# Gate/up of a SwiGLU block in 256-column chunks, partly issued between the groups of the inverse transform before it

## Chip, cores, metric

One core of a Trainium2 chip. The metric is device time in microseconds (us) of one execution; lower is better. A kernel repeated on one chip scatters mostly by 0.5%, at most by 0.8%, around its median, so versions are compared through ratios that were measured in the same rounds.

## The reference, cut to what matters

```python
# S = 2048 rows, D = 640, F = 1728, all bfloat16
h  = x + A(layernorm(x), k, v, ...)      # A: long convolution, done here with DFT matrices
xn = layernorm(h)
h2 = h + (silu(xn @ w_gate) * (xn @ w_up)) @ w_down
```

The convolution is computed as two forward transforms, products in the frequency domain and an inverse transform, all as matmuls against cosine and sine tables. Then comes the feed-forward block. Only the part from the inverse transform on is changed.

## The kernel before

The kernel places each instruction on one engine's in-order queue and lists the semaphore values that it waits for. PE does matmuls, DVE the elementwise work, ACT the activations. PE writes its results to PSUM, a memory in banks, from which DVE and ACT read them; a bank can be used again when they have. The inverse transform has 16 groups, one for each tile of 128 rows. One group is 32 matmuls (384 and 256 columns in turn), then `y_output` on DVE with one Sqrt on ACT, then, two groups later, five PE transposes of the normalized rows:

```python
for par in range(2):
    for tb in range(NT):                                   # 16 groups
        banks, ytok = inverse_group(gi, par, tb)           # PE: 32 matmuls
        if len(pend) >= 2:
            hn_transposes(*pend.pop(0), [4, 5, 6, 7], ...) # PE: 5 transposes, DVE: 1 copy
        y_output(qi, par, tb, banks, ytok)                 # DVE, one Sqrt on ACT
        pend.append((par, tb))
...
def y_output(...):                       # ... cut to the order of the DVE queue
    q  = (x - mean) * rstd               # 1
    d  = kv * D                          # 2
    s  = psum + d                        # 3, 4: frees the PSUM banks of the inverse
    o  = q * s ; h = x + o               # 5, 6
    bn_stats, bn_stats, bn_aggr          # 7 to 9
    Sqrt on ACT, then reciprocal         # 10
    hn = (h - mean2) * rstd2             # 11
```

After all 16 groups the feed-forward runs in two halves of 1024 rows. Gate/up tiles are 512 columns wide, with one PSUM bank for gate and one for up, three such pairs in turn. A down half starts only when all products of its half are there:

```python
def gate_up_half(par, ...):
    for fb in range(NFB):                # 14 blocks of features, the last one of 64
        for c in range(NUC):             # 2 tiles of 512 columns
            # PE: 5 gate matmuls in bank bG, 5 up matmuls in bank bU, alternating
            t_sg = act.op(... Sigmoid ..., deps=[lastG, ...])
            t_gs = dve.op(... gate * sigmoid ..., deps=[t_sg, ...])
            t_gu = dve.op(... up * that ..., deps=[t_gs, lastU])
...
gate_up_half(0) ; down_half(0) ; gate_up_half(1) ; down_half(1)
```

## Time and profile before

| | before |
|---|---|
| median at the time of the prediction | 491.54 us (4 runs) |
| inverse transform on PE | 204.6 to 290 us |
| gate/up and down, first half | 290.5 to 392 us |
| gate/up and down, second half | 392 to 487 us |

In the profile PE is the matmul engine. These lines of the kernel matter: L742 the inverse matmuls, L767 the DVE adds that free the banks of the inverse, L793 the transposes, L797 their copy, L848 and L850 the gate and up matmuls, L856 the sigmoid, L858 and L861 the two products, L891 the down matmuls, L777 the Sqrt.

The first lines of the page of the kernel before give the span and each engine's busy time:

```profile
span 490.2 us, 6781 instructions
...
PE 420.5 (86%) x2710; PEld 261.1 (53%) x2710; DVE 328.2 (67%) x624; ACT 133.6 (27%) x298; POOL 0.3 (0%) x5
```

The table by stretches, kernel before. The columns are the stretch, its length, the busy time of PE, PEld (weight loads), DVE, ACT and POOL with the number of instructions, the granted clock of PE as a share of full speed (0.50 is half clock), and DMA's share and GB/s. The stretches are the inverse, the hand-over to gate/up, the first down half and the second gate/up half:

```profile
204.60:290.50 85.90, 77.52 (x582) 54.89 (x582) 67.74 (x172) 4.12 (x14) 0.00 (x0) 0.98 0.32 109
290.50:302.00 11.50, 7.26 (x36) 3.17 (x37) 8.99 (x22) 3.45 (x6) 0.00 (x0) 1.00 0.01 1
...
358.30:392.00 33.70, 33.66 (x224) 21.30 (x224) 6.23 (x14) 0.00 (x0) 0.00 (x0) 0.95 0.10 35
392.00:454.80 62.80, 60.82 (x282) 27.49 (x281) 39.58 (x58) 16.70 (x28) 0.00 (x0) 1.00 0.01 4
```

In the hand-over PE is busy only 7.26 of 11.5 us. The clock of 0.95 in the first down half means a piece at half clock: (1 - 0.95) x 33.7 is 1.7 us lost.

The waits of PE from 204 us on, kernel before (total, times, longest). The first line is the stage before, which the change doesn't touch:

```profile
PE ps L742 <- DVE r_stage L693: 26.5, 1, 26.5
PE ps L742 <- DVE r_x L767: 7.9, 13, 0.8
PE ps L891 <- DVE tabs L861: 4.0, 2, 2.0
PE ps L848 <- DVE tabs L861: 2.9, 1, 2.9
PE ps L848 <- DVE r_k L797: 1.3, 1, 1.3
PE ps L848 <- DVE r_x L767: 0.6, 1, 0.6
```

Besides that first line PE waits 16.7 us: 7.9 in the inverse (DVE frees the banks too late), 4.8 at the hand-over, 4.0 before the two down halves. That is all that better overlap could win at the full clock. PE starts one inverse group every 5.37 us but has only 4.35 us of inverse matmuls and 0.28 us of transposes to do in it.

Two groups of DVE instructions with their mean time in ns give the cost of a narrower product: 691 at 512 columns, and 415 for an add of 256 columns that also reads PSUM (kernel before, groups by form):

```profile
L858 DVE TENSOR_TENSOR r_kpl<-ps,r_kpl 128x512 bf16<-128x512 f32 x52 | 36.0, 691 | 37.6 <-ACT r_kpl L856 37.6
...
L899 DVE TENSOR_TENSOR r_x<-ps,kvt 128x256 bf16<-128x256 f32 x16 | 6.6, 415 | 0.0
```

The timeline of ACT before the first Sqrt (start, duration, instruction) shows a table load of 1.28 us:

```profile
83.37 1.28 ACT L520 ACT_TABLE_LOAD   x1
84.66 0.32 ACT L520 ACTIVATE sqv<-lnstat,epsv 128x16 f32<-128x16 f32 x1
```

That Sqrt needs the last result of the convolution's input stage, which DVE finishes at 84.1 us. The load starts before that. It does not wait for the activation's operand.

### The profile page before, as it was taken

The page shows a single profiled execution, that of the slowest core. Times are in us where ns is not written, and L with a number is a line of the kernel's source. Part 1 is how long each engine was busy: PE and PEld are TensorE (multiplying, and loading weights), DVE is VectorE, ACT ScalarE, POOL GpSimd, SP SyncE. Part 2 cuts the span into 40 slices and gives each one's busy share as a digit, 9 for nine tenths or more (in the row PEclk, how much of TensorE's full clock was granted, in tenths as well). Part 3 has the DMA queues.
Part 4 walks back from the last instruction along what each step waited for, and adds up shares of the span by engine and source line. Part 5 has one row for each costly group of instructions (what it writes and reads, how often), then busy time and mean ns, then how long its engine had stood idle before and what let it go on. Part 6 is the DMA issues. An engine that isn't in the chain of part 4 may idle for free.

```text
span 490.2 us, 6781 instructions
## 1 busy us (share of the span) xinstructions
PE 420.5 (86%) x2710; PEld 261.1 (53%) x2710; DVE 328.2 (67%) x624; ACT 133.6 (27%) x298; POOL 0.3 (0%) x5
## 2 busy tenths in 40 slices
PE   2589998999998850398998987999989999999897
PEld 1456775677775530166666653444446644444564
DVE  0789998096499999748888888666622256666222
ACT  0843435655665550000000003222200022222000
POOL 0000000000000000000000000000000000000000
PEclk9888999899999985599999999999989999999999
DMA  8999710000000000294110100000001100000011
GB/s 296 348 350 345 226 66 2 0 1 1 1 1 1 0 1 1 68 408 134 41 28 27 30 25 1 1 1 0 1 14 42 40 15 0 2 0 1 27 41 40
DMA packets 24271, 32.22 MB, mean 66 GB/s; under 512 B 2800, under 2 KB 17968, under 8 KB 24240
## 3 DMA queue, kind: packets, MB, share of 16 engines
q1 hardware_dynamic: 21168, 25.16, 15.8%
q10 hardware_dynamic: 3072, 6.64, 3.6%
q8 instruction: 21, 0.34, 0.3%
q14 instruction: 10, 0.08, 0.1%
HBM read 29.16 MB, written 2.62 MB: 65 GB/s over the span
## 4 chain that ended last, share of the span: by engine, by line
PE 49%; DVE 39%; SPq 4%; issue 3%; ACT 2%; DMA 1%; DVEq 0%
PE ps L891 13%; PE ps L848 12%; DVE r_x L629 12%; PE ps L850 12%; PE ps L574 9%; SPq L311 4%; PE ps L742 3%; DVE r_x L767 3%; DVE r_stage L629 2%; DVE r_x L770 2%; DVE kvt L771 2%; DVE st L773 2%; DVE r_k L779 1%; DVE st L417 1%; DMA r_stage<-in_A_k_dram 1%
## 5 line engine op out<-in xcount | busy, mean ns | idle before, releaser
L848 PE MATMUL ps<-r_k,r_kpl 128*128 128x512 bf16 (+1 forms) x280 | 106.2, 379 | 4.8 <-DVE tabs L861 2.9
L850 PE MATMUL ps<-r_k,r_kpl 128*128 128x512 bf16 (+1 forms) x280 | 106.1, 379 | 0.0
L742 PE MATMUL ps<-r_stage,tabs 128*128 128x384 bf16 x480 | 71.7, 304 | 34.4 <-DVE r_stage L693 26.5
L742 PEld LDWEIGHTS ps<-r_stage,tabs 128*128 128x128 bf16 x480 | 46.6, 99 | 54.7 <-DVE r_stage L693 26.9
L574 PE MATMUL ps<-r_k,tabs 128*128 128x384 bf16 x480 | 70.0, 311 | 6.3 <-ACT r_k L543 4.3
L574 PE MATMUL ps<-kvt,tabs 128*128 128x384 bf16 x480 | 67.7, 304 | 7.0 <-ACT r_x L588 4.8
L891 PE MATMUL ps<-r_x,tabs 128*128 128x384 bf16 x448 | 66.0, 305 | 4.0 <-DVE tabs L861 4.0
L858 DVE TENSOR_TENSOR r_kpl<-ps,r_kpl 128x512 bf16<-128x512 f32 (+1 forms) x56 | 38.7, 691 | 40.9 <-ACT r_kpl L856 40.9
L856 ACT ACTIVATE r_kpl<-ps 128x512 bf16<-128x512 f32 (+1 forms) x56 | 33.2, 597 | 120.3 <-PE ps L848 120.3
L574 PEld LDWEIGHTS ps<-r_k,tabs 128*128 128x128 bf16 x480 | 48.4, 101 | 27.2 <-ACT r_k L543 4.5
L574 PEld LDWEIGHTS ps<-kvt,tabs 128*128 128x128 bf16 x480 | 47.4, 99 | 27.0 <-ACT r_x L588 5.4
L891 PEld LDWEIGHTS ps<-r_x,tabs 128*128 128x128 bf16 x448 | 41.9, 99 | 28.4 <-issue 8.9
L899 DVE TENSOR_TENSOR r_x<-ps,kvt 128x384 bf16<-128x384 f32 (+1 forms) x32 | 14.2, 486 | 53.9 <-PE ps L891 53.9
L629 DVE TENSOR_TENSOR r_x<-r_x 128x1280 bf16<-128x1280 bf16 x40 | 31.5, 820 | 25.5 <-ACT r_k L588 13.4
L848 PEld LDWEIGHTS ps<-r_k,r_kpl 128*128 128x128 bf16 (+1 forms) x280 | 27.6, 99 | 38.9 <-DVE tabs L861 4.2
L629 DVE TENSOR_TENSOR r_x<-r_x,r_kpl 128x2560 bf16<-128x2560 bf16 x32 | 46.2, 1486 | 0.3
L850 PEld LDWEIGHTS ps<-r_k,r_kpl 128*128 128x128 bf16 (+1 forms) x280 | 27.6, 99 | 31.8
L584 ACT ACTIVATE r_kpl<-ps,sck 128x384 bf16<-128x384 f32 x64 | 28.5, 528 | 44.1 <-PE ps L574 44.1
L861 DVE TENSOR_TENSOR tabs<-ps,r_kpl 128x512 bf16<-128x512 f32 (+1 forms) x56 | 38.7, 691 | 1.9
L777 ACT ACTIVATE sqv<-lnstat,epsv 128x1 f32<-128x1 f32 x16 | 4.7, 294 | 110.4 <-DVE lnstat L775 76.0
L584 ACT ACTIVATE r_x<-ps 128x384 bf16<-128x384 f32 x64 | 25.6, 454 | 33.3 <-PE ps L574 30.7
L588 ACT ACTIVATE r_x<-ps,tw 128x384 bf16<-128x384 f32 (+1 forms) x64 | 31.3, 565 | 0.0
(58 smaller groups left out, 249.2 us busy)
## 6 DMA issues: line engine op xcount, KB each, us to landing
r_stage<-in_A_k_dram SPq DMA_DIRECT2D x15, 320.0 KB, 5.1
r_k<-in_A_ssm_k_dram SPq DMA_DIRECT2D x5, 512.0 KB, 5.8
r_stage<-in_A_q_dram SPq DMA_DIRECT2D x8, 320.0 KB, 4.2
r_stage<-in_A_v_dram SPq DMA_DIRECT2D x8, 320.0 KB, 4.5
r_x<-in_A_q_dram SPq DMA_DIRECT2D x16, 160.0 KB, 2.2
out_dram<-r_x SPq DMA_DIRECT2D x16, 160.0 KB, 1.8
r_kpl<-in_B_w_gate_dram ACTq DMA_DIRECT2D x1, 2160.0 KB, 8.6
r_kpl<-in_B_w_up_dram ACTq DMA_DIRECT2D x1, 2160.0 KB, 13.9
```

Source lines behind the costliest of these rows:

```text
L311: return e.op_inc(lambda g, d=dst, s=src: g.dma_start(d, s), sem, 16, deps=deps)
L574: t.matmul(o, l, r, start=st, stop=sp_),
L584: atok = act.op(lambda a, o=dst, s=src, sc=sc: a.activation(out=o, in_=s, func=ACTF.Copy, scale=sc), deps=[last[gi]] + list(extra_act_deps))
L588: atok = act.op(lambda a, o=sdst[:, ch0:ch0 + cw], s=src[0:npart], sc=ssc: a.activation(out=o, in_=s, func=ACTF.Copy, scale=sc), deps=list ...
L629: tt = lambda o, a, b2, op, dd: dve.op(lambda v: v.tensor_tensor(out=o, in0=a, in1=b2, op=op), deps=dd)
L742: lasts[c] = pe.op(lambda t, o=o, l=lhsT, r=r, st=first, sp_=(cnt > nmm - NCH): t.matmul(o, l, r, start=st, stop=sp_), deps=deps if (first ...
L848: lastG = pe.op(lambda t, o=oG, l=lg, r=rhs, st=st, sp_=sp_: t.matmul(o, l, r, start=st, stop=sp_), deps=deps if dti == 0 else ())
L850: lastU = pe.op(lambda t, o=oU, l=lu, r=rhs, st=st, sp_=sp_: t.matmul(o, l, r, start=st, stop=sp_))
L856: t_sg = act.op(lambda a, o=sgb, s=oG: a.activation(out=o, in_=s, func=ACTF.Sigmoid), deps=[lastG, gu_pair_done.get(pidx - 3)])
L858: t_gs = dve.op(lambda v, o=gsb, s=oG, g=sgb: v.tensor_tensor(out=o, in0=s, in1=g, op=ALU.mult), deps=[t_sg, gu_pair_done.get(pidx - 3)])
L861: t_gu = dve.op(lambda v, o=dstgu, s=oU, g=gsb: v.tensor_tensor(out=o, in0=s, in1=g, op=ALU.mult), deps=[t_gs, lastU] + guT_war_deps)
L891: last = pe.op(lambda t, o=o, l=lhsT, r=r, st=first, sp_=(ft == NFB - 1): t.matmul(o, l, r, start=st, stop=sp_), deps=deps if (first and c ...
```

## The change

The intent is to give PE something to do while the inverse is bound by DVE. Gate/up is cut into eight chunks of 256 rows, and the rows of a chunk are ready as soon as two row tiles are transposed. In each inverse group from the fourth on, two gate/up blocks (one feature block of gate and up, 256 columns) are issued. After the inverse, one down chunk and 14 gate/up blocks alternate, with the blocks about 12 ahead of the down chunk that needs them. Gate and up now share one PSUM bank.

```diff
-    TUW = min(512, H)
+    TC = min(256, H)              # rows of a chunk; SBC = 2 row tiles
...
+        pair_banksets = [(b_, b_) for b_ in [4, 5, 6]]
...
+        def gu_emit(ci):          # next block of chunk ci; cut
+                oG = bank32(bG, 0, TC)[0:mrows]
+                oU = bank32(bU, TC, TC)[0:mrows]       # same bank, other half
+                lastG = pe.op(... t.matmul(o, l, r, start=st, ...))
+                lastU = pe.op(... t.matmul(o, l, r, start=False, ...))
+            t_sg = act.op(... Sigmoid ..., deps=[lastU, prev3])
+            t_gs, t_gu = dve.op(...), dve.op(...)
...
-        def y_output(qi, par, tb, banks, ytok):
+        def y_output(qi, par, tb, banks, ytok, between=lambda: None):
                 bank_rd[banks[c]] = t_s
+            between()             # here: between adds 3, 4 and product 5
...
+        GU_PER_GROUP = 2
+        NGSLOT = 2                # products of two chunks are held at a time
...
+                    hn_transposes(ppar, ptb, [7], tri[0])
+                t_h, t_hn = y_output(qi, par, tb, banks, ytok, between=lambda: emit_some_gu(GU_PER_GROUP))
...
+        while next_down < n_chunks:
+            # any block of this chunk still missing is emitted first (cut)
+            down_chunk(next_down)
+            downs_emitted[0] = next_down + 1
+            while pend:
+                ...
+                hn_transposes(ppar, ptb, [7], tri[0])
+            emit_some_gu(NFB)
+            next_down += 1
```

Two accumulations are open in one bank at once. The Trainium skill ("PSUM — Partial Sum Buffer", The four PSUM rules) says that only the first matmul issued there may carry the start flag, and that the second group, in other columns, overwrites at its first matmul without it. The change follows that.

More of the change, by code (lines that the diff above doesn't have):

```diff
@@ L139, in bass_sequential_preLN__ssm_conv_h3__swiglu_ffn__prompt_kernel @@
     assert FL in (32, 64, 128)
-    TUW = min(512, H)
-    assert H % TUW == 0
-    NUC = H // TUW
+    TC = min(256, H)
+    assert H % TC == 0 and TC % P == 0
+    NCC = H // TC
+    SBC = TC // P
+    TUW = TC
     half = D // 2
@@ L189, in bass_sequential_preLN__ssm_conv_h3__swiglu_ffn__prompt_kernel @@
         stab = tabs[:, NT * H:2 * NT * H].rearrange("p (t h) -> p t h", t=NT)
-        assert NFB * H <= 2 * NT * H
-        guT = tabs[:, 0:NFB * H].rearrange("p (f u) -> p f u", f=NFB)
         kvt = sb("kvt", [P, 2, NT, D], bf)
@@ L245, in bass_sequential_preLN__ssm_conv_h3__swiglu_ffn__prompt_kernel @@
         assert yoff <= sz_k, (yoff, sz_k)
-        sz_kpl = max(NF * 4 * D, 2 * NDT * F + 6 * TUW)
+        sz_kpl = max(NF * 4 * D, 2 * NDT * F + 6 * TUW + NFB * TC)
         r_kpl = sb("r_kpl", [P, sz_kpl], bf)
@@ L253, in bass_sequential_preLN__ssm_conv_h3__swiglu_ffn__prompt_kernel @@
         gsbuf = [r_kpl[:, sgoff + (3 + i) * TUW:sgoff + (4 + i) * TUW] for i in range(3)]
+        gcoff = sgoff + 6 * TUW
+        guC = [None, r_kpl[:, gcoff:gcoff + NFB * TC].rearrange("p (f u) -> p f u", f=NFB)]
         xt_elems = 2 * 6 * D + 2 * 4 * D + 2 * 2 * D + 4 * D
@@ L284, in bass_sequential_preLN__ssm_conv_h3__swiglu_ffn__prompt_kernel @@
             yoff2 += D
+        if yoff2 + NFB * TC <= r_x.shape[1]:
+            guC[0] = r_x[:, yoff2:yoff2 + NFB * TC].rearrange("p (f u) -> p f u", f=NFB)
+            yoff2 += NFB * TC
+        else:
+            guC[0] = sb("guC0", [P, NFB, TC], bf)[:, :, :]
         ps = es.enter_context(nc.psum_tensor("ps", [P, 8 * BANK], f32))
@@ L722, in bass_sequential_preLN__ssm_conv_h3__swiglu_ffn__prompt_kernel, with inverse_group @@
         ytmp_prev = {0: [], 1: []}
-        def inverse_group(gi, par, tb):
-            banks = [(gi % 2) * 2, (gi % 2) * 2 + 1]
+        def inverse_group(gi, par, tb, force_banks=None):
+            banks = force_banks if force_banks is not None else [(gi % 2) * 2, (gi % 2) * 2 + 1]
             deps = list(inv_deps_all)
@@ L806, in bass_sequential_preLN__ssm_conv_h3__swiglu_ffn__prompt_kernel @@
         tri = [0]
-        gi = 0
-        for par in range(2):
-            for tb in range(NT):
-                qi = gi
-                banks, ytok = inverse_group(gi, par, tb)
-                if len(pend) >= 2:
-                    ppar, ptb = pend.pop(0)
-                    hn_transposes(ppar, ptb, [4, 5, 6, 7], tri[0])
-                    tri[0] += 1
-                t_h, t_hn = y_output(qi, par, tb, banks, ytok)
-                h_tok[(par, tb)] = t_h
-                pend.append((par, tb))
-                if qi + NXR < len(y_order):
-                    x_reload(qi + NXR)
-                gi += 1
@@ L823, in bass_sequential_preLN__ssm_conv_h3__swiglu_ffn__prompt_kernel @@
-        gu_pair_done = {}
-        sg_prev = [None] * 3
-        pair_banksets = [(0, 1), (4, 5), (6, 7)]
-        def gate_up_half(par, pidx_start, tr_interleave):
-            pidx = pidx_start
-            u_half0 = par * H
-            hnT_deps = [hnT_tok[(par, tb)] for tb in range(NT)]
-            tri = 0
-            for fb in range(NFB):
-                mrows = P if fb < NFB - 1 else FL
-                for c in range(NUC):
-                    bset = pair_banksets[pidx % 3]
-                    bG, bU = bset
-                    deps = [t_wg, t_wu] + hnT_deps + [gu_pair_done.get(pidx - 3)]
-                    deps += [bank_rd.get(bG), bank_rd.get(bU), tr_bank_rd.get(bG), tr_bank_rd.get(bU)]
-                    lastG = lastU = None
-                    for dti in range(NDT):
-                        lg = Wg_sb[:, dti, fb * P:fb * P + mrows]
-                        lu = Wu_sb[:, dti, fb * P:fb * P + mrows]
-                        rhs = hnT[:, dti, u_half0 + c * TUW:u_half0 + (c + 1) * TUW]
-                        oG = bank32(bG, 0, TUW)[0:mrows]
-                        oU = bank32(bU, 0, TUW)[0:mrows]
-                        st = dti == 0
-                        sp_ = dti == NDT - 1
-                        lastG = pe.op(lambda t, o=oG, l=lg, r=rhs, st=st, sp_=sp_: t.matmul(o, l, r, start=st, stop=sp_),
-                                      deps=deps if dti == 0 else ())
-                        lastU = pe.op(lambda t, o=oU, l=lu, r=rhs, st=st, sp_=sp_: t.matmul(o, l, r, start=st, stop=sp_))
-                    sgi = pidx % 3
-                    sgb = sgbuf[sgi][0:mrows, :]
-                    gsb = gsbuf[sgi][0:mrows, :]
-                    oG = bank32(bG, 0, TUW)[0:mrows]
-                    oU = bank32(bU, 0, TUW)[0:mrows]
-                    t_sg = act.op(lambda a, o=sgb, s=oG: a.activation(out=o, in_=s, func=ACTF.Sigmoid),
-                                  deps=[lastG, gu_pair_done.get(pidx - 3)])
-                    t_gs = dve.op(lambda v, o=gsb, s=oG, g=sgb: v.tensor_tensor(out=o, in0=s, in1=g, op=ALU.mult),
-                                  deps=[t_sg, gu_pair_done.get(pidx - 3)])
-                    dstgu = guT[0:mrows, fb, c * TUW:(c + 1) * TUW]
-                    t_gu = dve.op(lambda v, o=dstgu, s=oU, g=gsb: v.tensor_tensor(out=o, in0=s, in1=g, op=ALU.mult),
-                                  deps=[t_gs, lastU] + guT_war_deps)
-                    gu_pair_done[pidx] = t_gu
-                    bank_rd[bG] = t_gs
-                    bank_rd[bU] = t_gu
-                    pidx += 1
-                if tr_interleave is not None and tri < len(tr_interleave):
-                    tr_interleave[tri]()
-                    tri += 1
-            while tr_interleave is not None and tri < len(tr_interleave):
-                tr_interleave[tri]()
-                tri += 1
-            return pidx
@@ L875, in down_half @@
-        def down_half(par, qstart):
-            q = qstart
-            gdeps = [gu_pair_done[k] for k in gu_pair_done]
-            wdep = [t_wd, t_wd2]
-            for tb in range(NT):
-                banks = [(q % 2) * 2, (q % 2) * 2 + 1]
-                deps = gdeps + wdep + [bank_rd.get(banks[0]), bank_rd.get(banks[NCH - 1])] + [tr_bank_rd.get(banks[0]), tr_bank_rd.get(banks[NCH - 1])]
+        chunk_list = [(par, cc) for par in range(2) for cc in range(NCC)]
+        gu_done = {}
+        pair_banksets = [(b_, b_) for b_ in [4, 5, 6]]
@@ new lines, in bass_sequential_preLN__ssm_conv_h3__swiglu_ffn__prompt_kernel, with chunk_ready @@
+        NSET = len(pair_banksets)
+        pidx_c = [0]
+        down_done = {}
+        gu_next_fb = {}
+        obuf_free = [None, None]
+        q_c = [0]
+        def chunk_ready(ci):
+            par, cc = chunk_list[ci]
+            return all((par, SBC * cc + sb) in hnT_tok for sb in range(SBC))
+        def gu_emit(ci):
+            fb = gu_next_fb.get(ci, 0)
+            if fb >= NFB:
+                return False
+            gu_next_fb[ci] = fb + 1
+            par, cc = chunk_list[ci]
+            pidx = pidx_c[0]
+            pidx_c[0] += 1
+            mrows = P if fb < NFB - 1 else FL
+            u0 = par * H + cc * TC
+            hdeps = [hnT_tok[(par, SBC * cc + sb)] for sb in range(SBC)]
+            bG, bU = pair_banksets[pidx % NSET]
+            slot = ci % 2
+            deps = [t_wg, t_wu] + hdeps + [gu_done.get((pidx - NSET, None))]
+            deps += [bank_rd.get(bG), bank_rd.get(bU), tr_bank_rd.get(bG), tr_bank_rd.get(bU)]
+            lastG = lastU = None
+            for dti in range(NDT):
+                lg = Wg_sb[:, dti, fb * P:fb * P + mrows]
+                lu = Wu_sb[:, dti, fb * P:fb * P + mrows]
+                rhs = hnT[:, dti, u0:u0 + TC]
+                oG = bank32(bG, 0, TC)[0:mrows]
+                oU = bank32(bU, TC, TC)[0:mrows]
+                st = dti == 0
+                sp_ = dti == NDT - 1
+                lastG = pe.op(lambda t, o=oG, l=lg, r=rhs, st=st, sp_=sp_: t.matmul(o, l, r, start=st, stop=sp_, skip_group_check=True),
+                              deps=deps if dti == 0 else ())
+                lastU = pe.op(lambda t, o=oU, l=lu, r=rhs, sp_=sp_: t.matmul(o, l, r, start=False, stop=sp_, skip_group_check=True))
+            sgi = pidx % 3
+            sgb = sgbuf[sgi][0:mrows, :]
+            gsb = gsbuf[sgi][0:mrows, :]
+            oG = bank32(bG, 0, TC)[0:mrows]
+            oU = bank32(bU, TC, TC)[0:mrows]
+            prev3 = gu_done.get((pidx - 3, None))
+            t_sg = act.op(lambda a, o=sgb, s=oG: a.activation(out=o, in_=s, func=ACTF.Sigmoid), deps=[lastU, prev3])
+            t_gs = dve.op(lambda v, o=gsb, s=oG, g=sgb: v.tensor_tensor(out=o, in0=s, in1=g, op=ALU.mult), deps=[t_sg, prev3])
+            dstgu = guC[slot][0:mrows, fb, :]
+            t_gu = dve.op(lambda v, o=dstgu, s=oU, g=gsb: v.tensor_tensor(out=o, in0=s, in1=g, op=ALU.mult),
+                          deps=[t_gs, lastU, down_done.get(ci - 2)])
+            gu_done[(pidx, None)] = t_gu
+            gu_done[(ci, fb)] = t_gu
+            bank_rd[bG] = t_gs
+            bank_rd[bU] = t_gu
+            return True
@@ new lines, in down_chunk @@
+        def down_chunk(ci):
+            par, cc = chunk_list[ci]
+            slot = ci % 2
+            gdeps = [gu_done[(ci, fb)] for fb in range(NFB)]
+            wdep = [t_wd, t_wd2]
+            last = None
+            for sb in range(SBC):
+                tb = SBC * cc + sb
+                q = q_c[0]
+                q_c[0] += 1
+                banks = [2 * sb, 2 * sb + 1] if SBC * 2 <= 4 else [(q % 2) * 2, (q % 2) * 2 + 1]
+                deps = gdeps + wdep + [bank_rd.get(b_) for b_ in banks] + [tr_bank_rd.get(b_) for b_ in banks]
@@ L882, in down_half @@
                 first = True
-                last = None
-                u0 = tb * P
+                u0 = sb * P
                 for ft in range(NFB):
                     krows_ = P if ft < NFB - 1 else FL
-                    lhsT = guT[0:krows_, ft, u0:u0 + P]
+                    lhsT = guC[slot][0:krows_, ft, u0:u0 + P]
                     for c, (ch0, cw) in enumerate(chunks):
@@ L903, in down_half, with emit_some_gu @@
                 obuf_free[q % 2] = otok
-                q += 1
-            return q
-        obuf_free = [None, None]
-        guT_war_deps = []
-        tr1 = [lambda t=t, k=k: hn_transposes(t[0], t[1], [2, 3], k) for k, t in enumerate(pend)]
-        pend = []
-        pidx = gate_up_half(0, 0, tr1)
-        q = down_half(0, 0)
-        guT_war_deps = []
-        pidx = gate_up_half(1, pidx, None)
-        q = down_half(1, q)
+            down_done[ci] = last
+        gi = 0
+        n_chunks = len(chunk_list)
+        cur_gu = [0]
+        GU_PER_GROUP = 2
+        NGSLOT = 2
+        downs_emitted = [0]
+        def emit_some_gu(nmax):
+            n = 0
+            while n < nmax and cur_gu[0] < n_chunks:
+                ci = cur_gu[0]
+                if ci >= downs_emitted[0] + NGSLOT or not chunk_ready(ci):
+                    break
+                if gu_emit(ci):
+                    n += 1
+                else:
+                    cur_gu[0] += 1
+            return n
+        for par in range(2):
+            for tb in range(NT):
+                qi = gi
+                banks, ytok = inverse_group(gi, par, tb)
+                if len(pend) >= 2:
+                    ppar, ptb = pend.pop(0)
+                    hn_transposes(ppar, ptb, [7], tri[0])
+                    tri[0] += 1
+                t_h, t_hn = y_output(qi, par, tb, banks, ytok, between=lambda: emit_some_gu(GU_PER_GROUP))
+                h_tok[(par, tb)] = t_h
+                pend.append((par, tb))
+                if qi + NXR < len(y_order):
+                    x_reload(qi + NXR)
+                gi += 1
+        next_down = 0
+        while next_down < n_chunks:
+            while gu_next_fb.get(next_down, 0) < NFB:
+                assert chunk_ready(next_down)
+                gu_emit(next_down)
+            if cur_gu[0] <= next_down:
+                cur_gu[0] = next_down + 1
+            down_chunk(next_down)
+            downs_emitted[0] = next_down + 1
+            while pend:
+                ppar, ptb = pend.pop(0)
+                hn_transposes(ppar, ptb, [7], tri[0])
+                tri[0] += 1
+            emit_some_gu(NFB)
+            next_down += 1
         sp.wait([s_out[0].cur(), s_out[1].cur()])
```

## The prediction

> **What bounds the kernel now.** Only the part from the inverse transform on (204.6 to 490.2 us) changes. Read from the chain of waits and the timeline:
> - inverse transform, 204.6 to about 296 us: bound by DVE. Each group takes 5.37 us, paced by DVE; PE needs 4.35 plus five transposes at 56 ns, and waits 0.6 to 0.8 per group. The hand-over to gate/up costs PE 2.9 and 1.3 us more.
> - gate/up twice, about 61 us each: bound by PE, matmuls of 512 columns 215 ns apart; DVE is busy 63% of it.
> - down twice, about 33 us each: bound by PE, 4.02 us per row tile. Before each, PE waits 2.0 us for the last gating product; half clock after one of them costs 1.7 us.
>
> **What the change does.** Gate and up go to 256 columns, in eight chunks of rows, and two feature blocks are issued per inverse group from the fourth group on: 26 of the 112 blocks, 28 us of PE work, move into the DVE-bound stage.
>
> Costs, from the trace:
> - PE: 256-column matmuls in the inverse start every 109 ns with their weight loads hidden: 1.09 us a block; gate/up grows by 2 to 4 us in all.
> - DVE: a product from PSUM takes 691 ns at 512 columns and 415 ns at 256 (the adds of that size). Two blocks add about 1.5 us per group; DVE becomes 5.37 + 1.5 = 6.87 us, PE 4.35 + 0.28 + 2.18 = 6.8. They almost balance.
> - ACT: Sqrt and Sigmoid now alternate. The Trainium skill ("ScalarE: Activation LUTs", What ACT_TABLE_LOAD costs) gives 1283 ns plus a drain of 1380 per switch. The trace shows 1283 and no drain before the sigmoids (the load starts 0.02 us after Sqrt ends). I expect about 26 loads, 33 us of ACT, but hidden: the load before the first Sqrt starts at 83.4 us, before its DVE input is ready at 84.1, so loads don't wait for the activation's operand, and ACT idles over 2 us before each Sqrt.
> - One PSUM bank per gate/up pair, three sets: release takes about 1.7 us, below the 2.2 us of the other two sets. No PE stall.
>
> **The sum.** Fourth group at 230.4 us, a stall of PE before it (225.1 to 229.7, waiting for the second transposed tile), perhaps followed by half clock (1.5 us); last group near 314 us; 1.5 us around the last transposes. Then 86 blocks (95 us) and 14 row tiles (56 us), one wait of 1.8 us before the last chunk instead of two, and the same 3.2 us tail: span about 484, time **485.5 us**, range 479 to 493. Faster by over 2%: 0.24; within 2%: 0.69; slower: 0.07.
>
> **What would show it.** Inverse groups 6.8 to 7.2 us apart; 256-column starts 109 ns apart; about 28 table loads, few on the chain; chain in the interleaved stage mixed PE and DVE; PE continuous from about 327 us to the last chunk; DVE busy up about 11 us.
>
> **What would make it wrong.** Table loads that wait for the operand: +1.3 us per group, total about 500; with the skill's drain more. PE stalls from three banks, or DVE and PE delaying each other: +5 us. More half clock through short idle times (the skill, "TensorE: Matmul & The Clock Gate", Part 1: idle PE is throttled; here 3.4 us at 0.5 after one wait).

## The result and the profile after

The changed kernel ran in 483.92 us (median of 11 runs, 480.42 to 485.71; a twelfth run, 486.26, outside this median) against 491.78 us before (16 runs). The ratio is 0.9827, with a 95% interval of 0.980 to 0.985. Ratios here and below are the mean time of one kernel's fast runs over that of the other's of the same rounds, so they are not quite the ratio of the quoted medians. The gain is 1.7%: within 2%, and within the predicted range of 479 to 493. The outputs are right.

In the changed kernel L749 is the inverse, L774 its adds, L801 and L805 the transposes and their copy, L854 and L856 gate and up, L863 the sigmoid, L864 and L866 the products, L894 down, L785 the Sqrt. The first lines of its page:

```profile
span 483.9 us, 8166 instructions
...
PE 422.8 (87%) x3270; PEld 316.2 (65%) x3270; DVE 342.9 (71%) x736; ACT 176.6 (37%) x380; POOL 0.3 (0%) x5
```

The waits of PE in the changed kernel, from 205 us on:

```profile
PE ps L749 <- DVE r_stage L700: 24.9, 1, 24.9
PE ps L854 <- DVE r_k L805: 4.3, 1, 4.3
PE ps L894 <- DVE r_kpl L866: 1.5, 1, 1.5
PE ps L801 <- DVE r_k L805: 1.1, 1, 1.1
PE ps L749 <- DVE r_x L774: 0.9, 1, 0.9
```

Without the first line PE waits 7.8 us instead of 16.7. The 13 waits inside the inverse, the hand-over and one of the two waits before down are gone. A new one stands at the top, 4.3 us: the first block waits for the copy of the second transposed tile, and behind it in PE's queue the next inverse group waits too.

The stretches of the changed kernel: the groups without blocks, the first group with blocks, the other twelve, and the alternating stage after the inverse:

```profile
205.90:231.00 25.10, 19.90 (x139) 13.77 (x140) 14.23 (x36) 2.17 (x4) 0.00 (x0) 0.91 0.82 298
231.00:236.40 5.40, 5.40 (x25) 3.54 (x25) 2.84 (x8) 1.40 (x3) 0.00 (x0) 0.50 0.00 0
236.40:317.60 81.20, 81.20 (x680) 63.84 (x679) 72.35 (x188) 42.50 (x59) 0.00 (x0) 1.00 0.09 24
...
327.50:470.90 143.40, 143.40 (x1200) 114.65 (x1196) 82.85 (x195) 32.53 (x85) 0.00 (x0) 1.00 0.05 16
```

In the second of these PE runs at half clock after its wait, which costs 2.7 us. In the third PE is busy for the whole stretch. DVE is nearly full too, busy 72.35 of 81.20 us: in a closer timeline its only regular wait is 0.36 us per group, for the Sqrt, as before. The groups start 6.81 us apart in PE's timeline.

The products and the two kinds of table load in the changed kernel (groups by form):

```profile
L864 DVE TENSOR_TENSOR r_kpl<-ps,r_kpl 128x256 bf16<-128x256 f32 x104 | 43.9, 423 | 23.6 <-ACT r_kpl L863 23.6
...
L863 ACT ACT_TABLE_LOAD x14 | 18.0, 1283 | 0.2
L785 ACT ACT_TABLE_LOAD x13 | 16.7, 1283 | 0.2
```

Where the loads stand, from the timeline of ACT over one group:

```profile
255.28 0.38 ACT L863 ACTIVATE r_kpl<-ps 128x256 bf16<-128x256 f32 x1 [0.34 <-PE ps L856]
256.38 0.38 ACT L863 ACTIVATE r_kpl<-ps 128x256 bf16<-128x256 f32 x1 [0.71 <-PE ps L856]
256.78 1.28 ACT L785 ACT_TABLE_LOAD   x1
260.17 0.29 ACT L785 ACTIVATE sqv<-lnstat,epsv 128x1 f32<-128x1 f32 x1 [2.11 <-DVE lnstat L783]
260.49 1.28 ACT L863 ACT_TABLE_LOAD   x1
262.09 0.38 ACT L863 ACTIVATE r_kpl<-ps 128x256 bf16<-128x256 f32 x1 [0.33 <-PE ps L856]
```

Each load starts 0.02 us after the activation before it, is over before its own activation may start, and is followed by a wait for PE or DVE. The room is not the same at both places: over the twelve groups the waits after a load are 1.8 to 2.3 us before the Sqrt, but mostly 0.3 us, and at least 0.16, before the sigmoid. 27 loads take 34.7 us of ACT and none of the critical path. A drain of 1380 ns, which the Trainium skill ("ScalarE: Activation LUTs", What ACT_TABLE_LOAD costs) adds to each switch, is not seen.

**The balance from the start of the inverse.** It lasts 285.6 us before (490.2 - 204.6) and 278.0 us after (483.9 - 205.9), 7.6 us less. To count PE's pauses in one way for both kernels, take every distance of more than 0.4 us between the starts of two successive matmuls and subtract what such a pair takes without a pause. (The waits view counts a bit less, since it lets a matmul's modelled end overlap the pause.) The sums are 19.5 us before and 8.4 us after.

| Term | us |
|---|---|
| PE's pauses | -11.1 |
| half clock: 1.7 before, 2.7 after, and 0.3 less at the very start | +0.7 |
| gate/up, from the starts of matmuls: 112 blocks of 1.107 us; before, the same work 1.082 us | +2.9 |
| down, in the same way: 63.9 in both | 0.0 |
| sum | -7.5 |

### The profile page after: what moved, and what is told of

Its sections match the earlier page's. It is cut to its first block, busy times and chain, and to the rows that moved or that the text cites. A ratio compares the mean times of both kernels' runs of the same rounds, so it can differ in the third digit from the quotient of the medians.

```text
span 483.9 us, 8166 instructions
## 1 busy us (share of the span) xinstructions
PE 422.8 (87%) x3270; PEld 316.2 (65%) x3270; DVE 342.9 (71%) x736; ACT 176.6 (37%) x380; POOL 0.3 (0%) x5
## 4 chain that ended last, share of the span: by engine, by line
PE 64%; DVE 27%; SPq 4%; issue 2%; DMA 1%; ACT 1%; DVEq 0%
PE ps L749 14%; PE ps L854 13%; PE ps L894 13%; PE ps L856 13%; DVE r_x L636 12%; PE ps L581 10%; SPq L318 4%; DVE r_stage L636 2%; DMA r_stage<-in_A_k_dram 1%; DVE st L424 1%; DVE r_stage L431 1%; DVE r_stage L433 1%; DVE r_stage L436 1%; DVE r_stage L437 1%; DVE r_stage L428 1%
## 5 line engine op out<-in xcount | busy, mean ns | idle before, releaser
L854 PE MATMUL ps<-r_k,r_kpl 128*128 128x256 bf16 (+1 forms) x560 | 126.3, 276 | 4.3 <-DVE r_k L805 4.3
L856 PE MATMUL ps<-r_k,r_kpl 128*128 128x256 bf16 (+1 forms) x560 | 126.1, 275 | 0.0
L749 PE MATMUL ps<-r_stage,tabs 128*128 128x384 bf16 x480 | 71.8, 304 | 25.8 <-DVE r_stage L700 24.9
L863 ACT ACTIVATE r_kpl<-ps 128x256 bf16<-128x256 f32 x112 | 42.9, 383 | 132.6 <-PE ps L856 132.6
L581 PE MATMUL ps<-kvt,tabs 128*128 128x384 bf16 x480 | 70.0, 310 | 8.9 <-ACT r_x L595 4.8
L749 PEld LDWEIGHTS ps<-r_stage,tabs 128*128 128x128 bf16 x480 | 47.4, 99 | 45.0 <-DVE r_stage L700 25.2
L581 PE MATMUL ps<-r_k,tabs 128*128 128x384 bf16 x480 | 68.5, 307 | 6.3 <-ACT r_k L550 4.3
L864 DVE TENSOR_TENSOR r_kpl<-ps,r_kpl 128x256 bf16<-128x256 f32 x112 | 47.3, 422 | 25.8 <-ACT r_kpl L863 25.8
L854 PEld LDWEIGHTS ps<-r_k,r_kpl 128*128 128x128 bf16 (+1 forms) x560 | 55.7, 99 | 14.9 <-issue 6.4
L856 PEld LDWEIGHTS ps<-r_k,r_kpl 128*128 128x128 bf16 (+1 forms) x560 | 55.8, 100 | 6.1
L894 PE MATMUL ps<-r_x,r_kpl 128*128 128x384 bf16 x224 | 32.3, 300 | 1.5 <-DVE r_kpl L866 1.5
L894 PE MATMUL ps<-r_x 128*128 128x384 bf16 x224 | 32.3, 300 | 0.0
L785 ACT ACTIVATE sqv<-lnstat,epsv 128x1 f32<-128x1 f32 x16 | 4.7, 294 | 71.7 <-DVE lnstat L783 37.5
L894 PEld LDWEIGHTS ps<-r_x,r_kpl 128*128 128x128 bf16 x224 | 20.8, 97 | 12.2 <-issue 3.2
```

Source lines behind the costliest of these rows:

```text
L581: t.matmul(o, l, r, start=st, stop=sp_),
L749: lasts[c] = pe.op(lambda t, o=o, l=lhsT, r=r, st=first, sp_=(cnt > nmm - NCH): t.matmul(o, l, r, start=st, stop=sp_), deps=deps if (first ...
L854: lastG = pe.op(lambda t, o=oG, l=lg, r=rhs, st=st, sp_=sp_: t.matmul(o, l, r, start=st, stop=sp_, skip_group_check=True), deps=deps if dt ...
L856: lastU = pe.op(lambda t, o=oU, l=lu, r=rhs, sp_=sp_: t.matmul(o, l, r, start=False, stop=sp_, skip_group_check=True))
L863: t_sg = act.op(lambda a, o=sgb, s=oG: a.activation(out=o, in_=s, func=ACTF.Sigmoid), deps=[lastU, prev3])
L864: t_gs = dve.op(lambda v, o=gsb, s=oG, g=sgb: v.tensor_tensor(out=o, in0=s, in1=g, op=ALU.mult), deps=[t_sg, prev3])
```

## The experiments

Ratios are against the kernel before of the same rounds; diffs are against the changed kernel unless said otherwise. The theories at the start:

- **A**: the gain is the interleaving, PE work moved into a stage bound by DVE.
- **B**, a rival: interleaving is nearly free of net gain, since its first block waits 4.3 us and then runs at half clock. The gain is the order by chunks, which removes the waits at the hand-over and before down.
- Beside these: what the narrow tiles cost, and whether the table loads are really hidden.

| Run | Median, us | Ratio (95%) |
|---|---|---|
| no interleaving | 495.17 | 1.004 (1.000 to 1.008) |
| blocks from the fifth group on | 479.43 | 0.973 (0.969 to 0.976) |
| narrow tiles alone | 494.81 | 1.004 (1.000 to 1.008) |
| table loads exposed | 500.42 | 1.016 (1.011 to 1.020) |
| ends filled | 477.11 | 0.969 (0.966 to 0.973) |
| 12 blocks in the last six groups | 489.34 | 0.994 (0.990 to 0.998) |
| 12 blocks in groups five to ten | 490.94 | 0.997 (0.993 to 1.001) |
| changed kernel again | 484.21 | 0.983 (0.980 to 0.987) |
| bridge | 488.00 | 0.989 (0.985 to 0.994) |
| blocks from the fifth group on, again | 479.33 | 0.971 (0.968 to 0.975) |
| bridge, ready in time | 483.15 | 0.982 (0.980 to 0.985) |

### No interleaving

```diff
-        GU_PER_GROUP = 2
+        GU_PER_GROUP = 0
...
+        emit_some_gu(26)          # the same blocks, right after the inverse
         next_down = 0
```

> The changed kernel, but no gate/up block is issued inside the inverse transform; the same 26 blocks follow directly after it, in the same order, so that everything later is unchanged. Theory A (the gain is the interleaving: PE work moved into the stage bound by DVE): the 26 blocks come back as 29 us behind an inverse stage of 5.37 us per group, and the time returns to that of the kernel before or more, 491 to 494 us. Theory B (read from the gaps between matmuls: most of the gain is the order by chunks, which removes the waits at the hand-over, 4 us, and before the two down stages, 4.5 us and 1.7 us of half clock, and the interleaving gives nearly nothing net, since its first block waits 4.4 us and then runs at half clock): 485 to 487 us, with inverse groups 5.37 us apart and no PE wait over 2 us except one before the last chunk.

It took 495.17 us, slightly more than the kernel before. Theory B, which I held at that point, is wrong. The waits of PE in this kernel around the hand-over:

```profile
PE ps L854 <- DVE r_x L866: 7.8, 1, 7.8
```

and the stretch after that wait:

```profile
297.30:302.70 5.40, 5.34 (x26) 3.78 (x27) 2.79 (x8) 0.77 (x2) 0.00 (x0) 0.50 0.00 0
```

The hand-over did not vanish with the order by chunks; it grew. ACT and DVE take their queues in order, so the sigmoids and products of these blocks stand behind the Sqrt and the DVE work of the last two row tiles. PE fills its three banks (3.3 us of work) and then waits 7.8 us for the first of them, after which half clock costs 2.7 us. In the kernel before, the three bank pairs held twice as much work, and its longest such wait was 2.9 us. So the interleaving earns its keep, but not only by filling idle time inside the inverse; the runs below look at the hand-over.

### Blocks from the fifth group on

```diff
-                ... between=lambda: emit_some_gu(GU_PER_GROUP))
+                ... between=lambda: emit_some_gu(GU_PER_GROUP if qi >= 4 else 0))
```

> The changed kernel, with the first blocks issued in the fifth inverse group instead of the fourth (24 blocks inside the stage instead of 26). If the 4.4 us wait of PE before its first block and the half clock after it are a loss on the critical path, as I think, the wait goes and PE runs on: 3 to 6 us less than the changed kernel, 478 to 481 us, no gap over 1.2 us between matmuls of 215 to 320 us and no stretch at half clock there. If the stage is bound by DVE from there on, so that the wait is hidden, the time stays within 1 us of the changed kernel, 483 to 485.

It took 479.43 us, as expected on the side of "the wait is on the critical path". The same kernel, repeated in later rounds, gave 0.971. One condition in the emission loop wins another 1% over the changed kernel, whose ratio is 0.983. In the trace the wait for the second transposed tile is gone. These waits of PE are left:

```profile
PE ps L801 <- DVE r_k L805: 2.1, 1, 2.1
PE ps L894 <- DVE r_kpl L866: 1.5, 1, 1.5
PE ps L749 <- DVE r_x L774: 0.6, 1, 0.6
```

The first two lie after the inverse. Up to its end no wait of PE is over 1 us, and from 208 to 317 us PE runs at full clock.

### Narrow tiles alone

The diff is against the kernel before:

```diff
-    TUW = min(512, H)
+    TUW = min(256, H)
```

> The kernel before, with gate/up in tiles of 256 columns instead of 512 and nothing else changed. This is the cost of the narrower tile by itself: 109 ns instead of 215 per matmul, and more waits of PE on DVE, 112 instead of 56 blocks: 3 to 4 us longer than the kernel before, 494 to 496 us, the two gate/up stages about 62.5 us instead of 61. If the weight loads or the gating on DVE (77 to 93 us) limited the narrow tiles, it would be over 6 us longer.

It took 494.81 us, ratio 1.004: by the ratio 1.8 us more than the kernel before, less than the 3 to 4 expected and not clear of zero (the interval starts at 0.9996). The second gate/up half, which no other effect disturbs, takes 61.3 us instead of 60.6, both with PE busy throughout. So the narrow matmuls as such cost 0.7 us per half, less than the 1.5 I expected; 256 columns are enough to hide each weight load. At the hand-over the longest wait went from 2.9 to 4.5 us and was followed by 6.1 us at half clock, while the two waits before down shrank from 4.0 to 2.7 us; I have not taken these apart further.

### Table loads exposed

```diff
             t_sg = act.op(... Sigmoid ...)
+            if gi < NT * 2 and pidx % 2 == 0:       # first block of an inverse group
+                act.op(lambda a: a.activation(out=dumv[:], in_=epsv[:], func=ACTF.Sqrt, ...))
             t_gs = dve.op(...)
```

> The changed kernel, with one dummy Sqrt of one column between the two sigmoids of each inverse group (one group in two blocks). It adds two table loads of 1.28 us and 0.3 us per group at a place where DVE waits for the second sigmoid. If the table loads are free in the changed kernel only because ACT has idle time where they fall, as predicted, the groups go from 6.81 us to 8.2 to 8.8 us apart and the time to 498 to 508 us, with DVE waiting for the second sigmoid. If a table load cost nothing wherever it stands (it overlaps with other ACT work), the time stays within 1 us of the changed kernel.

It took 500.42 us, 16 us more than the changed kernel, and groups start 8.4 us apart. The timeline of ACT and DVE in this kernel over the blocks of one group (line numbers are one to three higher; L866 holds the dummy Sqrt, L867 the first product):

```profile
278.90 0.38 ACT L864 ACTIVATE r_kpl<-ps 128x256 bf16<-128x256 f32 x1
279.30 1.28 ACT L866 ACT_TABLE_LOAD   x1
...
280.60 0.29 ACT L866 ACTIVATE dumv<-epsv 128x1 f32<-128x1 f32 x1
...
280.91 1.28 ACT L864 ACT_TABLE_LOAD   x1
282.20 0.38 ACT L864 ACTIVATE r_kpl<-ps 64x256 bf16<-64x256 f32 x1
...
282.61 0.42 DVE L867 TENSOR_TENSOR r_kpl<-ps,r_kpl 64x256 bf16<-64x256 f32 x1 [1.48 <-ACT r_kpl L864]
```

The second sigmoid is 3.3 us after the first, and DVE waits 1.48 us for it in this group. Two more loads with the dummy Sqrt (0.29 us) cost 1.6 us per group. The loads of the changed kernel are therefore not free as such; they cost nothing because they fall into idle time of ACT.

### Ends filled

The diff is against the version that starts in the fifth group:

```diff
             down_chunk(next_down)
             downs_emitted[0] = next_down + 1
+            emit_some_gu(NFB if next_down != n_chunks - 3 else NFB + 4)
             while pend:
                 ... hn_transposes(ppar, ptb, [7], tri[0]) ...
-            emit_some_gu(NFB)
```

> The later start (blocks from the fifth group on), with two more waits of PE filled: the last two row tiles are transposed after the next 14 gate/up blocks instead of before them (a wait of 2.3 us and a stretch of half clock that cost 1.7 us), and the last four blocks of the last chunk are issued before the last down chunk but one (a wait of 1.7 us). If PE is the bound of everything after the fifth group, as I now hold, all three come off the time: 4 to 5.5 us less than the later start, 474 to 476 us, about 0.963 of the kernel before. If DVE or the clock sets the pace there, under 2 us.

It took 477.11 us: 0.969, 3.1% less than the kernel before and the lowest ratio here. By the ratios (0.969 against 0.973 and 0.971 in other rounds) that is 1 to 2 us better than the later start, not 4 to 5.5, and the intervals overlap, so a gain over the later start is not shown. By its size this is the branch that I had given to DVE or the clock; but in the trace PE is busy for 162.59 of the 164.1 us from 307.9 to 472.0 us and DVE for 95.93, so PE is still the bound there, and what failed is the saving that I had counted. The waits of PE that are left, this kernel:

```profile
PE ps L749 <- DVE r_stage L700: 26.5, 1, 26.5
PE ps L801 <- DVE r_k L805: 1.5, 1, 1.5
PE ps L749 <- DVE r_x L774: 0.6, 1, 0.6
```

The wait before the last down chunk is gone. The wait between the last two transposes only moved: both use bank 7, so the second waits for the copy of the first wherever the pair stands. And the half clock that I had counted, 1.7 us in the trace of the later start, was absent from the trace of the same kernel when it was repeated, after the same wait of 2.1 us. So the saving expected from it was not a steady one (what decides on half clock is shown further down).

### Twelve blocks, late or early

The diff is against the version that starts in the fifth group, the first condition for one run and the second for the other:

```diff
-                ... if qi >= 4 else 0
+                ... if qi >= 10 else 0            # the last six groups
+                ... if 4 <= qi < 10 else 0        # groups five to ten
...
+        emit_some_gu(12)
         next_down = 0
```

> The later start, but only the last six inverse groups host blocks (12 instead of 24); the other 12 blocks follow right after the inverse. Both theories lose the idle time of PE in six groups, 0.7 us each, 4.2 us. Theory C (the hosted blocks also ease the hand-over, since their sigmoids and products stand among the work of the last row tiles in the in-order queues of ACT and DVE): the hand-over still costs one wait of about 3.4 us and some half clock, 483 to 488 us in all.

> The same count of hosted blocks, 12, but in the groups five to ten; none in the last six. Theory C: as without any interleaving, the blocks after the inverse find their sigmoids behind the Sqrt of the last two row tiles and their products behind their DVE work, so PE runs three blocks (its three banks) and waits about 8 us, followed by half clock worth 3 to 5 us: 489 to 494 us, 4 to 9 us over the run that hosts them in the last six groups. If only the number of hosted blocks counts (theory A: idle PE time filled), both runs have the same time within 1 us.

They took 489.34 and 490.94 us, the first above the 483 to 488 expected. Their intervals overlap, so the expected 4 to 9 us between them did not come. The waits at the hand-over are as expected; blocks in the last six groups:

```profile
PE ps L854 <- DVE r_x L866: 4.8, 2, 3.4
```

and blocks in groups five to ten:

```profile
PE ps L854 <- DVE r_x L866: 7.6, 1, 7.6
```

But the half clock evened it out in the two traces: in the first run it lasted 9.1 us, with a second pause in it, and in the second run PE had only 3.3 us of it after its longer wait. In sum each lost about 9 us at the hand-over (pauses of 5.2 and 7.8 us between matmul starts, and half clock worth about 4 and 1.6 us). Both lost most of the gain, although twelve blocks were hosted in each. So a place near the end is not what protects the changed kernel; whether the count is, these two runs cannot say, as both host 12. What the changed kernel has and these two lack is a down chunk right behind the inverse, instead of more blocks. The next runs test that.

### Bridge

Against the version that starts in the fifth group: all 14 blocks of the first chunk stand in the last seven groups, then the first down chunk follows directly, then 26 blocks.

```diff
-                ... if qi >= 4 else 0
+                ... if qi >= 9 else 0
...
-            emit_some_gu(NFB)
+            emit_some_gu(NFB if next_down else NFB + 12)
```

> The later start, but only the last seven inverse groups host blocks: 14, all of the first chunk, so that its down chunk can follow the inverse directly; then 26 blocks, and everything later in the order of the changed kernel. Against the run with blocks in the last six groups it hosts only two blocks more, but the first work of PE after the inverse is the down chunk, which needs nothing that is still queued on ACT or DVE. If this bridge is what spares the changed kernel the hand-over loss of about 9.5 us (wait and half clock) that both runs with 12 blocks showed, no PE wait over 2.5 us follows the inverse, and only the 0.7 us of idle PE in five more groups are lost against the later start: 0.978 to 0.984 of the kernel before, 481 to 485 us. If the loss comes from hosting few blocks, as such, it stays near those runs, 0.99 or more.

> The later start once more, to share a chip with the run above: 0.970 to 0.976 of the kernel before.

488.00 us, ratio 0.989: missed. The wait of PE behind the inverse:

```profile
PE ps L894 <- DVE r_x L866: 5.3, 1, 5.3
```

My edit had defeated its purpose: the last two products that the down chunk needs stand in the last group, and PE is about one group ahead of DVE when it comes to them. The down chunk was there but not ready. The later start in the same rounds gave 0.971.

### Bridge, ready in time

The same, with the 14 blocks in groups 8 to 14, so that the last two groups host none:

```diff
-                ... if qi >= 9 else 0
+                ... if 7 <= qi < 14 else 0
```

> As the bridge run, but the 14 blocks of the first chunk stand in groups 8 to 14 and the last two groups host none, so that the products that the down chunk needs are done when PE comes to it (in the bridge run they were still queued on DVE, a wait of 5.6 us). Hosted blocks: the same 14; position: earlier, which in the pair of runs with 12 blocks made the wait after the inverse longer. If readiness of the down chunk is what bridges the hand-over, no wait over 2.5 us follows the inverse, and the time is 0.976 to 0.984 of the kernel before (the later start with 0.7 us lost in each of five groups). If hosting in the last groups is what counts, a wait of 5 us or more stays, and 0.987 or more.

483.15 us, ratio 0.982, inside the expected range. The wait of PE behind the inverse, now for the bank that the last row tile frees:

```profile
PE ps L894 <- DVE r_x L774: 2.5, 2, 1.3
```

No half clock followed. The count of hosted blocks is the same as in the bridge run and their place is earlier, yet the loss at the hand-over is gone. An early place alone does not do it: the run with blocks in groups five to ten lost 7.6 us there. So what bridges the hand-over is a piece of PE work that needs nothing still queued on ACT or DVE. In the changed kernel the first down chunk is that piece: its products were finished six groups before.

### The changed kernel again

> The changed kernel once more, so that it and the other versions share a chip and the runs of the kernel before: 0.980 to 0.986 of the kernel before.

484.21 us, ratio 0.983: the result repeats in the rounds of the other versions. Its trace again has a wait of PE (4.5 us from one matmul start to the next) before the first block, and half clock after it.

## Why the prediction was right

- **Time.** Predicted 485.5 us, measured 483.92. The range and the class (within 2%) hold.
- **What bounds the kernel before**: right. The pauses of PE and the half clock that it named are the ones that went away.
- **Costs of the narrow tile**: right. PE starts 109 ns apart; gate/up grew by 2.9 us ("2 to 4"), of which the tiles alone explain 1.4 us (two halves of 0.7). A product took 423 ns against the 415 taken from the adds. DVE's busy time grew by 14.7 us, where I had said about 11.
- **Balance of the interleaved stage**: right. Groups are 6.81 us apart (6.8 to 7.2), with PE busy throughout and DVE nearly so. The chain there (followed back from the last instruction, at each step to what released it) is PE alone, not PE and DVE mixed as I wrote.
- **Table loads**: right, and tested. 27 loads ("about 26" in one place, "about 28" in another), none waiting for an operand, none on the chain. The fear of +1.3 us per group was sound: 1.6 us per group is what two loads in the wrong place cost.
- **Three banks for gate and up**: right. In the interleaved stage and in the alternating one PE never waits for a bank: it is busy throughout both.
- **The stall before the first block and half clock after it**: right in kind. The wait was 4.3 us (4.6 said) and the half clock 2.7 us (1.5 said). I had listed this as a cost; that it could be avoided by starting one group later, and is worth 5 us, came from the experiment.
- **The end**: a wait of 1.5 us before the last down chunk (1.8 said), and 1.1 us around the last transposes (1.5 said).

What the prediction did not say, and what I then first read wrongly (theory B), is why the hand-over disappears. The sum simply had no wait there, without a reason, so that this term came out right was luck: without interleaving the same chunks wait 7.8 us there, and in the bridge run, with interleaving, PE waits 5.3. The runs show that this is not a property of chunks or of interleaving as such, but of the ready down chunk behind the inverse.

Half clock follows some pauses of PE and not others of the same length. The clock records of the kept traces show what decides it. In each trace the granted clock changes only on a grid of 3.41 us, and the place of the grid against the start of the kernel differs from trace to trace. The two waits of 2.0 us before the down halves, kernel before, in stretches of its grid (columns as above):

```profile
355.10:358.50 3.40, 1.41 (x7) 0.57 (x6) 2.27 (x4) 0.59 (x1) 0.00 (x0) 1.00 0.01 2
358.50:362.00 3.50, 3.50 (x15) 2.06 (x14) 0.00 (x0) 0.00 (x0) 0.00 (x0) 0.51 0.00 0
450.70:454.10 3.40, 2.12 (x10) 0.88 (x8) 2.16 (x4) 0.97 (x2) 0.00 (x0) 1.00 0.00 0
454.10:457.50 3.40, 2.69 (x20) 1.96 (x21) 0.57 (x1) 0.00 (x0) 0.00 (x0) 1.00 0.00 0
```

The first wait lies within one stretch: PE is idle for 1.99 of 3.40 us, and the next stretch is at half clock. The second wait is split into 1.28 and 0.71 us by the edge of the grid, and the clock stays. The two traces of the later start differ in the same way: 2.11 us idle in one stretch, or 1.06 and 1.02 in two. In the 13 kept traces, from 204 us on, half clock followed each of the 11 stretches at full clock with 1.99 us or more of idle PE, and none of the 992 with 1.84 or less. (Earlier in the kernels, stretches with 1.95 to 2.02 us went both ways.) So whether a pause of 2 to 4 us brings half clock depends on where it falls on the grid. After such a pause, half clock seen in one trace, or missing there, says nothing about the version.

Not tested: a version without any Sqrt on ACT, which would take the table switches away altogether.

## What to carry to other kernels

When work is moved into a stage bound by another engine, add up both engines per step. The gain ends where they balance, and the first moved piece must be ready when it is issued, because everything behind it in the in-order queue waits too. Where one stage hands over to the next, put work there that depends on nothing still queued on the other engines; more work of the dependent kind only fills the PSUM banks and then waits. A switch of activation table (1.28 us here) cost nothing where ACT was idle, and two of them cost 1.6 us per group where DVE waited for ACT, so look at where the loads fall, not at their number.

## What the Trainium skill lacked or had wrong

- "ScalarE: Activation LUTs", What ACT_TABLE_LOAD costs: 1283 ns per load agrees exactly. The further drain of about 1380 ns per switch is not seen: loads started 0.02 us after the activation before them, 27 times, and activations that were ready started as soon as the load ended (within 0.02 us in the kernel with exposed loads). The page also doesn't say that a load need not wait for the operand of the activation that it stands before (83.37 us against an operand ready at 84.1 us), which is what lets it hide.
- "TensorE: Matmul & The Clock Gate", HAM oscillation: its rule is "no PE-idle gaps >~3.4µs". Here pauses of 2.3 to 2.4 us between matmul starts were followed by half clock twice (kernel before at 358 us, later start at 317 us), and were not in two other cases (kernel before at 454 us, the later start repeated), nor was one of 3.3 us (kernel before at 299 us). So a pause under 3.4 us is not safe: 1.99 us of idle PE within one 3.41 us stretch of the clock's grid was enough.
